# Hashed attention with a mixture of adapters: q and k turned by VectorE and by DMAs that move partitions, in place of TensorE transposes

## The chip, the cores and the metric

The kernel runs on one core of a Trainium2 chip. A core has five engines with queues of their own: TensorE (PE; its weight loads are listed as PEld), VectorE (DVE), ScalarE (ACT), GpSimd (POOL), and SyncE (SP), which here only issues transfers. PE writes its products to PSUM, a small memory of eight banks; everything else lies in SBUF, 128 partitions wide. Each engine executes its instructions in the order of its queue, and waits at an instruction until what that needs is there.

The metric is the time on the device in microseconds (us). All times below are of one core.

## The reference

There are two stages. The first is attention in which a query sees only the keys with the same hash. For 4 batches and 8 heads, 768 positions and 64 features:

```
bit    = (q . proj > 0)            6 bits each for q and for k; the 6 bits are the bucket
scores = q . k^T / 8               where the buckets are equal, else -1e9
attn   = softmax(scores)
out    = attn . v
```

The outputs of the 8 heads are put side by side: 3,072 rows of 512. The second stage routes each row to two of eight small adapters of rank 16:

```
logits = x @ w_gate ;  top 2 of 8 ;  w = exp(logit - max) / (sum + 1e-9)
out    = x + sum over the two of  w * ((x @ A[e]) @ B[e])
```

## The kernel before

The work is cut into 16 **head pairs** (two heads of one batch, numbered p), four to a batch. A pair's scores are a matrix of 768 keys by 768 queries for each of two heads, computed as nine **tiles** of 1,024 columns (`score`, s = 0 to 8). The equality of buckets is folded into the same product: `aug` holds, for q and for k, 64 rows of features and below them six rows of bits as plus or minus one half, and a constant row, so that one product with 71 rows gives the score less a large number where bits differ. ACT turns each tile from PSUM (two buffers, `ps_s`) into exponentials, `P`, in bf16 (line 193). `pvmm` then multiplies `P` with v (and a column of ones for the sum), and `norm` divides (lines 223 and 225) into `x`.

`aug` must have features on partitions, while q and k come from memory with positions on partitions. So each pair needs these steps, done one pair ahead:

- `load` (SP): q, k and v of a pair, 384 KB each. Partition number is position divided by six.
- `trans`, three times: four TensorE transposes of 128 by 128 in fp32 into one PSUM buffer (`ps_t`, two of them; line 144), and a DVE copy into `qkT` (line 147).
- `hash`: four products of `qkT` with the projection into one PSUM buffer (line 155), a DVE step that makes signs of them (`sgn`, line 158), and eight DMAs on SP that put the six bit rows of each of four parts into `aug` (line 164).
- `cast`, twice: DVE scales half of `qkT` and writes it to `aug` as bf16 (line 172).

There are two `aug` buffers, so the one for pair p+1 is filled while the scores of pair p are computed. GpSimd casts v to bf16 (`vcast`) and `x` to `xb` (line 229).

When a batch is done, the adapters follow: `xtrans` (TensorE transposes of `xb`, and a copy), `lgz` (logits and `x @ A` in one product), `route` (a chain of some ten short DVE steps and one exponential), `zmtrans`, and six times `delta` (a product with B, line 301, a DVE step that scales and adds, line 303, and every second time a store to memory). All of these share one PSUM buffer, `ps_m`.

The order is written out by hand in `run`: for each pair the nine score tiles, and after each tile some of the other work, for the pair before (values, normalisation), for the pair after (turning, hashing) and, through `moe_slot`, for the last batch. Each engine's queue has the instructions in that order. DVE's first work in a pair is the first normalisation of the pair before, `norm(p - 1, 0)`, and then the copies for pair p+1. SP has, for each pair, the three loads of pair p+2, then the eight bit DMAs of pair p+1, and in some pairs stores.

Of the kernel before, what the change touches and what calls it, by code (L numbers as in the profile page):

```python
# [19 lines left out]
class Emitter:  # L20


    def __init__(self, ctx, tc, q, k, v, proj, w_gate, A, Bm, out):
# [21 lines left out]
        self.qktp = ctx.enter_context(tc.tile_pool(name="qktp", bufs=2))  # L45
# [6 lines left out]
        self.ps_s = ps("ps_s", 2)  # L52
        self.ps_t = ps("ps_t", 2)
# [10 lines left out]
        self.proj2 = sg.tile([P, 32], F32, name="proj2")  # L64
        nc.vector.memset(self.proj2, 0.0)
        nc.sync.dma_start(out=self.proj2[0:64, 0:6], in_=proj)
        nc.sync.dma_start(out=self.proj2[64:128, 6:12], in_=proj)
# [5 lines left out]
        for i in range(2):  # L73
            a = sg.tile([P, 4, S], BF16, name=f"aug{i}")
            for h in range(2):
                nc.vector.memset(a[64:96, 2 * h, :], 1.0)
                nc.vector.memset(a[64:96, 2 * h + 1, :], -1.5)
            self.aug.append(a)
# [13 lines left out]
        self.nat, self.vn, self.qkT, self.sgn, self.P_, self.pv = {}, {}, {}, {}, {}, {}  # L92
# [13 lines left out]

    def load(self, p):
# [4 lines left out]
        n = self.natp.tile([self.P, 2, 2, self.T * self.D], F32, tag="nat", name=f"nat{p}")  # L112
        for i, src in enumerate((self.q, self.k)):
            nc.sync.dma_start(out=n[:, i], in_=src[b, h:h + 2].rearrange(
                "h (p t) d -> p h (t d)", t=self.T))
# [18 lines left out]

    def trans(self, p, g):
        if p >= self.n_pairs:
            return
        nc, P, D = self.nc, self.P, self.D
        if g == 0:
            self.qkT[p] = self.qktp.tile([P, 2 * self.S], F32, tag="qkT", name=f"qkT{p}")  # L140
        ps = self.ps_t.tile([P, 512], F32, tag="t", name=f"tr{p}_{g}")
        for j in range(4):
            idx, u = divmod(4 * g + j, 3)
            nc.tensor.transpose(out=ps[:, j * P:(j + 1) * P],  # L144
                                in_=self.nat[p][:, idx % 2, idx // 2, u * P:(u + 1) * P],
                                identity=self.ident)
        nc.vector.tensor_copy(out=self.qkT[p][:, g * 512:(g + 1) * 512], in_=ps)  # L147

    def hash(self, p):
        if p >= self.n_pairs:  # L150
            return
        nc = self.nc
        ps = self.ps_t.tile([self.P, 384], F32, tag="t", name=f"hs{p}")
        for j in range(4):
            nc.tensor.matmul(out=ps[32 * j:32 * j + 32, :], lhsT=self.proj2,  # L155
                             rhs=self.qkT[p][:, j * 384:(j + 1) * 384], start=True, stop=True)
        sgn = self.sgp.tile([self.P, 384], BF16, tag="sgn", name=f"sgn{p}")
# [3 lines left out]
        for j in range(4):  # L161
            av = aug[64:70, j, :].rearrange("p (u e c) -> p u e c", e=2, c=self.P)
            for e in range(2):
                nc.sync.dma_start(out=av[:, :, e, :],  # L164
                                  in_=sgn[32 * j + 6 * e:32 * j + 6 * e + 6, :].rearrange(
                                      "p (u c) -> p u c", c=self.P))

    def cast(self, p, e):
        if p >= self.n_pairs:
            return  # L170
        av = self.aug[p % 2][0:64].rearrange("p j (u e c) -> p (j u) e c", e=2, c=self.P)
        self.nc.vector.tensor_scalar(  # L172
            out=av[:, :, e, :],
            in0=self.qkT[p][64 * e:64 * e + 64, :].rearrange("p (j c) -> p j c", c=self.P),
            scalar1=2.0 ** -5, scalar2=None, op0=ALU.mult)


    def score(self, p, s):
# [6 lines left out]
        while at < end:  # L185
# [4 lines left out]
            nc.tensor.matmul(out=ps[:, o:o + n], lhsT=aug[0:71, 2 * h + 1, kt * P:(kt + 1) * P],  # L190
                             rhs=aug[0:71, 2 * h, q0:q0 + n], start=True, stop=True)
# [104 lines left out]
    def delta(self, b, i):  # L296
# [8 lines left out]
        if i % 2 == 1:  # L305
            S = self.S
            nc.sync.dma_start(
                out=self.out[b * S:(b + 1) * S, :].rearrange("(p t) f -> p t f", t=self.T)[:, i - 1:i + 1, :],
                in_=self.acc[b][:, i - 1:i + 1, :])


    def moe_slot(self, p, s):
        o = p - 2
        if o >= 0 and o % self.PPB == 0 and o // self.PPB >= 1:
            b = o // self.PPB - 1
            if s in (1, 3):
                self.lgz(b, s // 2)
            if s in (2, 4):
                self.route(b, s // 2 - 1)
            if s == 5:  # L320
                self.zmtrans(b)
        o = p - 3
        if o >= 0 and o % self.PPB == 0 and o // self.PPB >= 1:
            b = o // self.PPB - 1
            if s < 6:
                self.delta(b, s)

    def run(self):
# [3 lines left out]
        for g in range(3):  # L332
            self.trans(0, g)
        self.hash(0)
        self.cast(0, 0)
        self.cast(0, 1)
        self.vcast(0)
        self.load_moe()
        self.trans(1, 0)
        for p in range(N):  # L340
            for s in range(9):
                self.score(p, s)
                if s == 0:
                    self.load(p + 2)
                    self.norm(p - 1, 0)
                    self.trans(p + 1, 1)
                if s == 1:
                    self.trans(p + 1, 2)
                    self.vcast(p + 1)
                if s == 2:  # L350
# [79 lines left out]
```

The softmax here doesn't subtract the row's maximum and nothing guards it: scores larger than these inputs give would overflow.

## Time and profile before

| | |
|---|---|
| three runs, median | 218.93 us (218.74 to 220.49) |
| the profiled execution | 218.24 us, of which its span is 216.4 |
| PE clock granted, mean | 0.925 |
| ACT starts its first score tile | 18.83 |
| ACT ends its last score tile | 191.76 |
| PE / DVE / ACT / POOL busy | 178.0 / 142.9 / 144.1 / 63.4 us |
| ACT's wait for score tiles | 43.6 us |

The span is the time from the first to the last instruction in the trace; the rest of the device's time lies around it. Lines of the profile name an engine, a line of the code (L193 is line 193), an operation, what it writes and reads (`P<-s`), the shapes, how often it ran, its busy time and the mean duration of one in ns. Behind that stands the time for which the engine had been idle just before, with the instruction that released it. `SPq` is SP issuing a DMA; a line `DMA` in the chain of waits is the time until the data landed. Busy times overlap between engines, so a share says little by itself: what bounds a stretch is the engine for which the others wait there.

### The profile page before, as it was taken

Reading aid. Unit: us, or ns where it says so; the run is one execution under the profiler, and the core shown is the slowest. Engines: PE = TensorE matmul, PEld = TensorE weight load, DVE = VectorE, ACT = ScalarE, POOL = GpSimd, SP = SyncE. Lnnn points to the kernel's source line nnn. Section 1 sums busy time; section 2 is a strip of 40 time slices with the busy share of each in tenths; the row PEclk is TensorE's granted clock in tenths of the full one; section 3 lists DMA queues with packets and bytes.
Section 4 is the critical chain, followed back from the end, with each engine's and each line's share of the span. In section 5 each row is a group of like instructions: output and inputs, shape, how many; then the busy total and the mean of one; then the engine's idle time right before and its main releaser. Section 6 shows DMA issues by size and latency. Waiting matters only on the chain.

```text
span 216.4 us, 5569 instructions
## 1 busy us (share of the span) xinstructions
PE 178.0 (82%) x2288; PEld 123.5 (57%) x2288; DVE 142.9 (66%) x303; ACT 144.1 (67%) x153; POOL 63.4 (29%) x98
## 2 busy tenths in 40 slices
PE   1647999999999997998979987989999879774341
PEld 0314286865868674756656866657678656463200
DVE  7771528675686768698756689796766875634541
ACT  2003679998999987677969976868999858730000
POOL 1694420623416050604133503305144110101000
PEclk9995569999999999999999999999999999997555
DMA  5895406062442616180746042533815000420024
GB/s 144 293 25 82 169 11 217 9 224 71 160 156 76 224 22 209 9 309 11 253 168 215 15 152 76 191 132 141 283 46 186 3 9 3 197 100 0 0 118 173
DMA packets 22874, 26.39 MB, mean 122 GB/s; under 512 B 8897, under 2 KB 21313, under 8 KB 22849
## 3 DMA queue, kind: packets, MB, share of 16 engines
q1 hardware_dynamic: 18016, 25.77, 35.2%
q0 software_dynamic: 4832, 0.27, 3.9%
q8 instruction: 18, 0.29, 0.6%
q14 instruction: 8, 0.06, 0.1%
HBM read 19.42 MB, written 6.29 MB: 119 GB/s over the span
## 4 chain that ended last, share of the span: by engine, by line
PE 52%; DVE 22%; DMA 9%; SPq 8%; issue 5%; ACT 2%; POOLq 0%; POOL 0%; DVEq 0%
PE s L190 20%; PE pv L209 12%; SPq L164 7%; PE tr L144 7%; PE hs L155 5%; DVE acc L303 5%; DMA nat<-in_k_dram 5%; PE dl L301 3%; DMA aug<-sgn 3%; DVE aug L172 3%; DVE sgn L158 2%; PE xtp L238 2%; DVE zm L276 2%; DMA nat<-in_q_dram 2%; DVE x L225 2%
## 5 line engine op out<-in xcount | busy, mean ns | idle before, releaser
L193 ACT ACTIVATE P<-s 128x1024 bf16<-128x1024 f32 x144 | 141.6, 1024 | 47.1 <-PE s L190 43.6
L190 PE MATMUL s<-aug 71*128 71x512 bf16 (+1 forms) x384 | 89.9, 336 | 5.0 <-DMA aug<-sgn 4.8
L209 PEld LDWEIGHTS <-P 128*128 128x128 bf16 x1152 | 51.3, 98 | 14.8 <-DVE x L225 1.0
L209 PE MATMUL pv<-vb,P 128*128 128x65 bf16 x1152 | 53.8, 194 | 0.9 <-DVE x L225 0.9
L190 PEld LDWEIGHTS <-aug 71*128 71x128 bf16 x384 | 32.5, 100 | 28.8 <-issue 13.0
L229 POOL CAST xb<-x 128x768 bf16<-128x768 f32 x16 | 13.2, 825 | 115.3 <-DVE x L225 115.3
L147 DVE COPY qkT<-tr 128x512 f32<-128x512 f32 x48 | 33.0, 690 | 14.1 <-PE tr L144 12.5
L144 PE MATMUL tr<-ident,nat 128*128 128x128 f32 x192 | 32.9, 296 | 8.1 <-DMA nat<-in_q_dram 3.9
L209 PE MATMUL pv<-vb,eps 128*128 128x65 bf16 x192 | 37.4, 195 | 0.0
L144 PEld LDWEIGHTS tr<-ident,nat 128*128 128x128 f32 x192 | 25.2, 152 | 14.4 <-issue 5.6
L172 DVE TENSOR_SCALAR aug<-qkT 64x1536 bf16<-64x1536 f32 x32 | 31.9, 998 | 0.9
L223 DVE RECIPROCAL ri<-pv 128x6 f32<-128x6 f32 x32 | 6.2, 193 | 29.5 <-PE pv L209 29.4
L303 DVE SCALAR_TENSOR_TENSOR acc<-dl,rt,x 128x512 f32<-128x512 f32 x24 | 17.9, 745 | 6.0 <-PE dl L301 6.0
L209 PEld LDWEIGHTS <-eps 128*128 128x128 bf16 x192 | 18.9, 98 | 0.0
L225 DVE TENSOR_TENSOR x<-pv,ri 128x384 f32<-128x384 f32 x32 | 17.8, 557 | 1.2
L126 POOL CAST vb<-vn 128x768 bf16<-128x768 f32 x16 | 13.3, 833 | 13.7 <-DMA vn<-in_v_dram 13.7
L128 POOL TENSOR_TENSOR vs<-vn 128x384 f32<-128x384 f32 x16 | 16.7, 1044 | 0.0
L301 PE MATMUL dl<-Bcat,zmT 128*128 128x512 bf16 x24 | 10.3, 431 | 7.7 <-DVE acc L303 6.8
L155 PE MATMUL hs<-qkT,proj 128*32 128x384 f32 x128 | 15.8, 542 | 0.0
L158 DVE TENSOR_SCALAR sgn<-hs 128x384 bf16<-128x384 f32 x16 | 8.9, 558 | 8.6 <-PE hs L155 7.0
L250 PE MATMUL lz<-wa,xT 128*128 128x136 bf16 x96 | 7.7, 235 | 4.3 <-DVE zm L276 3.6
L238 PE MATMUL xtp<-ident_bf,xb 128*128 128x128 bf16 x96 | 8.0, 219 | 3.0 <-POOL xb L229 1.4
(35 smaller groups left out, 79.6 us busy)
## 6 DMA issues: line engine op xcount, KB each, us to landing
nat<-in_q_dram SPq DMA_DIRECT2D x16, 384.0 KB
nat<-in_k_dram SPq DMA_DIRECT2D x16, 384.0 KB
vn<-in_v_dram SPq DMA_DIRECT2D x16, 384.0 KB
out_dram<-acc SPq DMA_DIRECT2D x12, 512.0 KB
aug<-sgn SPq DMA_DIRECT2D x128, 4.5 KB
wa<-in_moe_A_dram POOLq DMA_DIRECT2D x4, 32.0 KB, 3.1
Bcat<-in_moe_B_dram POOLq DMA_DIRECT2D x1, 128.0 KB, 3.5
proj<-in_proj_dram SPq DMA_DIRECT2D x2, 1.5 KB
```

What stands on the lines that cost most here:

```text
L128: nc.gpsimd.tensor_add(out=s3, in0=vn[:, :, 0:3, :], in1=vn[:, :, 3:6, :])
L144: nc.tensor.transpose(out=ps[:, j * P:(j + 1) * P], in_=self.nat[p][:, idx % 2, idx // 2, u * P:(u + 1) * P], identity=self.ident)
L147: nc.vector.tensor_copy(out=self.qkT[p][:, g * 512:(g + 1) * 512], in_=ps)
L155: nc.tensor.matmul(out=ps[32 * j:32 * j + 32, :], lhsT=self.proj2, rhs=self.qkT[p][:, j * 384:(j + 1) * 384], start=True, stop=True)
L164: nc.sync.dma_start(out=av[:, :, e, :], in_=sgn[32 * j + 6 * e:32 * j + 6 * e + 6, :].rearrange("p (u c) -> p u c", c=self.P))
L172: self.nc.vector.tensor_scalar(out=av[:, :, e, :], in0=self.qkT[p][64 * e:64 * e + 64, :].rearrange("p (j c) -> p j c", c=self.P), scalar1 ...
L190: nc.tensor.matmul(out=ps[:, o:o + n], lhsT=aug[0:71, 2 * h + 1, kt * P:(kt + 1) * P], rhs=aug[0:71, 2 * h, q0:q0 + n], start=True, stop=True)
L193: nc.scalar.activation(out=self.P_[p][:, s * 1024:end], in_=ps, func=ACT.Exp, scale=128.0)
L209: nc.tensor.matmul(out=pv[:, i, :], lhsT=lhsT, rhs=vb[:, h, kt, :], start=(kt == 0), stop=(kt == T))
L225: nc.vector.tensor_tensor(out=self.x[b][:, :, c:c + D], in0=pv[:, :, 0:D], in1=ri.unsqueeze(2).to_broadcast([P, T, D]), op=ALU.mult)
L301: nc.tensor.matmul(out=ps, lhsT=self.zmT[b][:, i * P:(i + 1) * P], rhs=self.Bcat, start=True, stop=True)
L303: nc.vector.scalar_tensor_tensor(out=self.acc[b][:, i, :], in0=ps, scalar=self.rt[b][:, i:i + 1], in1=self.x[b][:, i, :], op0=ALU.mult, op ...
```

## The change

q and k are loaded with 12 neighbouring positions on a partition, the first head on partitions 0 to 63, the second on 64 to 127. `trans` is one DVE transpose for q and one for k, which turns each 32 by 32 block in its place and writes position order with a step of 12. `hash` multiplies the result with a projection laid out four times over (`proj4`), summing two products of 32 features. `cast` moves to GpSimd, which writes bf16 to a new tile `cb`; after the second cast of a pair, eight DMAs on SP bring blocks of 32 partitions to their place in `aug`. The bits go by four DMAs instead of eight. Positions in `aug` are now in natural order, so the score product reads its weights, the keys, with a step of six, and the output is stored with 128 rows to a block.

The PSUM buffers of `trans` go, and there are three score buffers; `hash` uses `ps_m`. In `run`, `trans` and `cast` stand behind tiles 0 and 1, the values of the second head behind tiles 1 to 3, `hash` behind tile 4, `xtrans` comes a pair earlier, and the adapters of a batch are spread over three pairs instead of two.

```diff
-        self.qktp = ctx.enter_context(tc.tile_pool(name="qktp", bufs=2))
+        self.tbp = ctx.enter_context(tc.tile_pool(name="tbp", bufs=2))
...
-        self.ps_s = ps("ps_s", 2)
-        self.ps_t = ps("ps_t", 2)
+        self.ps_s = ps("ps_s", 3)
...
+        for b in range(4):
+            nc.scalar.dma_start(out=pst[32 * b:32 * b + 32], in_=proj.rearrange("(d r) n -> r d n", d=2))
+        for b in range(4):
+            nc.vector.tensor_copy(out=self.proj4[32 * b:32 * b + 32, :, b:24:4], in_=pst[32 * b:32 * b + 32])
...
             nc.sync.dma_start(out=n[:, i], in_=src[b, h:h + 2].rearrange(
-                "h (p t) d -> p h (t d)", t=self.T))
+                "h (p t) d -> (h p) (t d)", t=2 * self.T))
...
+    def trans(self, p, i):
+        nc, P, T2 = self.nc, self.P, 2 * self.T
+        if i == 0:
+            self.tb[p] = self.tbp.tile([P, 2, 2, 32 * T2], F32, tag="tb", name=f"tb{p}")
+        nc.vector.transpose(
+            out=self.tb[p][:, :, i, :].rearrange("p d (c t) -> p t d c", t=T2),
+            in_=self.nat[p][:, i, :].rearrange("p (t d r) -> p t d r", t=T2, d=2))
+
+    def cast(self, p, i):
+        nc, P, T2 = self.nc, self.P, 2 * self.T
+        if i == 0:
+            self.cb[p] = self.tbp.tile([P, 2, 2, 32 * T2], BF16, tag="cb", name=f"cb{p}")
+        nc.gpsimd.tensor_scalar(out=self.cb[p][:, :, i, :], in0=self.tb[p][:, :, i, :],
+                                scalar1=2.0 ** -5, scalar2=None, op0=ALU.mult)
+        n = 32 * T2
+        if i == 1:
+            for d in range(2):
+                for b in range(4):
+                    h, b2 = divmod(b, 2)
+                    nc.sync.dma_start(
+                        out=self.aug[p % 2][32 * d:32 * d + 32, :, h, b2 * n:b2 * n + n],
+                        in_=self.cb[p][32 * b:32 * b + 32, d])
+
     def hash(self, p):
+        n = 16 * 2 * self.T
+        ps = self.ps_m.tile([P, n], F32, tag="m", name=f"hs{p}")
+        for d in range(2):
+            for g in range(4):
+                i, half = divmod(g, 2)
+                nc.tensor.matmul(out=ps[32 * g:32 * g + 32, :], lhsT=self.proj4[:, d, :],
+                                 rhs=self.tb[p][:, d, i, half * n:half * n + n],
+                                 start=(d == 0), stop=(d == 1))
...
+        for g in range(4):
+            i, half = divmod(g, 2)
+            nc.sync.dma_start(
+                out=aug[64:70, i].rearrange("r h (b x) -> r (h b) x", b=2)[:, :, half * n:half * n + n],
+                in_=sgn[32 * g:32 * g + 24, :])
...
-            nc.tensor.matmul(out=ps[:, o:o + n], lhsT=aug[0:71, 2 * h + 1, kt * P:(kt + 1) * P],
-                             rhs=aug[0:71, 2 * h, q0:q0 + n], start=True, stop=True)
+            nc.tensor.matmul(out=ps[:, o:o + n], lhsT=aug[0:71, 1, h, bass.ds(kt, P, step=self.T)],
+                             rhs=aug[0:71, 0, h, q0:q0 + n], start=True, stop=True)
...
     def moe_slot(self, p, s):
+        for k in (1, 2, 3):
+            o = p - k
+            if o < 0 or o % self.PPB != self.PPB - 1:
+                continue
+            b = o // self.PPB
+            if k == 1 and s == 5:
+                self.lgz(b, 0)
+                self.route(b, 0)
+            if k == 2 and s == 0:
+                self.lgz(b, 1)
+                self.route(b, 1)
+            if k == 2 and s == 5:
                 self.zmtrans(b)
+            if k == 3 and s in (0, 1, 2, 3, 5, 6):
+                self.delta(b, (0, 1, 2, 3, 5, 6).index(s))
...
                 if s == 0:
                     self.load(p + 2)
                     self.norm(p - 1, 0)
+                    self.trans(p + 1, 0)
+                    self.cast(p + 1, 0)
+                if s in (1, 2, 3):
+                    self.pvmm(p - 1, 1, 2 * s - 2, 2 * s)
+                if s == 1:
                     self.trans(p + 1, 1)
+                    self.cast(p + 1, 1)
+                if s == 3:
+                    self.norm(p - 1, 1)
+                if s == 4:
+                    self.hash(p + 1)
+                    self.vcast(p + 1)
+                if s == 5:
+                    self.xtrans(p - 1)
+                if s in (6, 7, 8):
+                    self.pvmm(p, 0, 2 * s - 12, 2 * s - 10)
                 self.moe_slot(p, s)
```

## The prediction

> **What bounds the kernel now.** I read the busy times first, then the costliest groups, then stretches of the loop by engine, then the chain of waits. Busy times and groups:
>
> ```profile
> PE 178.0 (82%) x2288; PEld 123.5 (57%) x2288; DVE 142.9 (66%) x303; ACT 144.1 (67%) x153; POOL 63.4 (29%) x98
> ...
> L193 ACT ACTIVATE P<-s 128x1024 bf16<-128x1024 f32 x144 | 141.6, 1024 | 47.1 <-PE s L190 43.6
> ...
> L126 POOL CAST vb<-vn 128x768 bf16<-128x768 f32 x16 | 13.3, 833 | 13.7 <-DMA vn<-in_v_dram 13.7
> L128 POOL TENSOR_TENSOR vs<-vn 128x384 f32<-128x384 f32 x16 | 16.7, 1044 | 0.0
> ```
>
> ACT waits 43.6 us for score tiles, so PE sets the pace. The stretches (busy by engine, then PE clock, DMA share, GB/s) are two plain head pairs of the loop, and the start:
>
> ```profile
> 13.20:17.20 4.00, 0.00 (x0) 0.03 (x1) 3.10 (x3) 0.00 (x0) 4.00 (x5) 0.94 1.42 36
> 17.20:22.00 4.80, 4.39 (x16) 2.71 (x17) 1.30 (x2) 2.05 (x2) 1.35 (x3) 0.50 0.47 113
> 22.00:26.00 4.00, 4.00 (x17) 1.24 (x16) 2.44 (x4) 2.43 (x3) 1.24 (x2) 0.50 0.51 191
> ...
> 50.80:59.80 9.00, 9.00 (x135) 6.62 (x134) 5.98 (x11) 8.59 (x9) 2.76 (x4) 1.00 0.43 137
> 59.80:69.00 9.20, 9.20 (x136) 6.74 (x135) 6.48 (x11) 8.61 (x10) 3.46 (x6) 1.00 0.40 135
> ```
>
> In a plain pair PE has no gap (9.00 of 9.00), but ACT is nearly full too: nine tiles back to back take 9.04 us (54.77 to 63.81 in the timeline). So taking work from PE can win a plain pair almost nothing. What lies above 9.04 is elsewhere: counted by ACT's tiles, the loop runs from 18.83 to 191.76, 172.9 us; pair 0 takes 13.1 and the pairs that carry adapter work 11 to 13. The third thing is how close pair 3 came to being late, in the chain of waits:
>
> ```profile
> 44.38 0.57 DVE sgn L158
> 44.95 0.02 issue
> 44.97 0.76 SPq L164
> 45.73 0.05 issue
> 45.78 0.73 SPq L164
> 46.51 0.05 issue
> 46.56 0.72 SPq L164
> 47.29 0.04 issue
> 47.33 3.07 DMA aug<-sgn
> 50.40 0.05 issue
> 50.45 0.28 PE s L190
> ```
>
> SP issues one sign DMA each 0.775 us, and the fourth lands 3.07 us after its issue began: the next pair's scores already wait for it. Loads are cheaper on the same queue (start to start 0.49 to 0.56):
>
> ```profile
> 51.22 0.44 SPq L114 DMA_DIRECT2D nat<-in_q_dram  x1
> 51.71 0.46 SPq L114 DMA_DIRECT2D nat<-in_k_dram  x1
> ```
>
> **The change by parts.** *PE.* Twelve transposes per head pair go, four of them 0.44 us in the chain, so 1.32 us: PE's work in a plain pair, W, falls from 9.0 to 7.7. Hashing streams as many columns as before. The score weights are now read with a step of six elements; no row has that. Bounds: nothing, or, by the fp32 weight load (140 ns against 98), 24 x 0.05 = 1.2 us per pair. I take nothing, since weight loads run beside matmuls.
>
> *DVE.* Per pair three copies (0.69) and two casts (0.95) go, 4.0 us, and two transposes of 128x768 fp32 come. Bounds for one: 0.55 (the cast's 954 ns for 1536 elements, halved, and a start) and 1.75 (a 512-element copy out of PSUM takes 0.69, so 768 take 0.95; that with the scattered write costing as much again). I take 0.95. DVE is free for a third of a plain pair, so its total is worth nothing; its place in order is what counts.
>
> *POOL.* Two casts of 768 elements per pair: 0.83 by its own cast, 2.1 by its two-input row (1.044 for 384). I take 0.83; they fit (POOL is busy 3 to 4 of 9 us).
>
> *SP.* Eight sign DMAs become four, still onto six rows (0.775 each), and eight partition-moving DMAs come, of 32 rows. Bounds 0.43 (the v load, 0.41, plus the gap) and 0.775; I take the loads' 0.49, since their shape is nearest. Per pair 8 x 0.49 + 4 x 0.775 + 1.5 for loads = 8.5 us: below the period, but serial. Data: 393 KB more per pair beside 1,180 KB that keep the DMA engines 40% busy; hidden. Loads in runs of 3,072 bytes and stores in runs of 2,048 I count at nothing, beside the same 40%.
>
> *Moves.* Hashing now takes the one small PSUM buffer, which the x transposition also uses one slot later: the sign step (about 0.4) releases it during a score tile of 0.44, so 0 to 0.4, and I take 0. The x transposition comes a pair earlier, two slots after the value products end: normalisation 0.78 and POOL's cast 0.83 need 1.6 us, and PE has 2.2 us of work between. Nothing, as long as POOL is not behind.
>
> **The new path.** All twelve DMAs must land before the pair's first score. They begin with DVE's transposes, which stand in DVE's order behind the first normalisation of the pair before, and that waits for PE's last matmuls of that pair. From there, L:
> - normalisation 0.20 + 0.56 and gaps: 0.83
> - two transposes: 1.98 with gaps
> - second POOL cast: 0.93
> - eight issues on SP: 3.92
> - three sign issues 2.33, the fourth's issue and landing 3.07, and the semaphore 0.05
> - sum **L = 13.1 us**; low ends together 11.5, high ends 18.5.
>
> The old path had only three issues before its last one. Call S(p) the start of pair p's scores on PE. S(p) + W is where PE ends pair p; there the normalisation begins, and L with it, for pair p+2. So S(p+2) is the later of S(p+1) + W and S(p) + W + L: two pairs cost 7.7 + 13.1 = 20.8, or 10.4 each, with PE idle 5.4 us in every second pair. The three score buffers don't help, since what they would hold is not computed yet. Behind SP's wait for POOL's cast stand the sign DMAs and the next loads (loads are a pair ahead, so nobody misses them); behind PE's wait at the first score stand the value products and the next hashing.
>
> *Adapter pairs*, three batches. In the first of the three pairs PE has 1.4 us more (a routing product 0.71, and a wait for the copy before it 0.65). In the second, routing stands on DVE between the two transposes and waits for a product behind the first score: S + 0.45 + 0.71 + 2.06 (routing, as in the tail, 197.6 to 199.6) + 0.95 + 0.93 + 3.92 + 2.33 + 3.12 = 14.5 from one start to the next, with no second pair to share it. In the third, the first accumulation (0.38 + 0.75) stands there instead and two output issues (0.45 each) come before the signs: 13.8.
>
> Intervals: pair 0 13.1 as before; 13.1, 7.7, 13.1; then 9.1, 14.5, 13.8, 8.3; then 12.5, 14.5, 13.8, 8.3; then 12.5, 14.5, 13.8, and 9.0 for the last, which ACT bounds. (8.3 and 12.5 follow from the rule: the third adapter pair's W is 9.0, so 9.0 + 13.1 - 13.8 = 8.3 and 20.8 - 8.3 = 12.5.) Sum 191.6, against 172.9: **+18.7**.
>
> *Start.* DVE is free at 8.0; small copies for the projection 0.4 (estimate from the 0.09 us memset), transposes to 10.3, cast to 11.2, SP to 15.1, landing at 20.6, first tile at half clock 1.06: ACT starts at 21.7 instead of 18.83, **+2.8**. *Tail*: one transposition of x leaves it, but it ran while PE waited for the last normalisation; 0.
>
> *Clock.* After PE idled 4.0 us (13.2 to 17.2) its clock was 0.50 until about 30, and pair 0 took 4 us more than others; a 1.6 us idle at 110 left the clock at 1.00. The new stalls are 5 us. If each costs the next pair 4 us, the same intervals give +17 instead of +0 (adapter pairs absorb most). I take a quarter, **+4**: behind the stalls work is dense, at the start it was not. The Trainium skill (TensorE: Matmul & The Clock Gate, Part 1) says idle of about 3.4 us halves the clock and as long a busy stretch restores it; the row's low clock lasted longer. By that rule a stalled pair loses about 1.7 us, +7 in all, an estimate from the page.
>
> Sum: the profiled execution took 218.24 (span 216.4), 0.3% under the median 218.93. 218.24 + 18.7 + 2.8 + 4 = **244**.
>
> A rule of the skill speaks against the change: the SBUF Cachelines section of Advanced Engine Details and Errata wants two accesses in each 16-byte line. The transposes write at a step of 48 bytes and the score weights are read at 12. No row here shows either; by the rule both lean to their upper ends.
>
> **Rivals.**
> - *Dear steps* (chance 0.20): SP's new issues cost the signs' 0.775. L becomes 15.3, and some ten intervals lengthen by about 2: 264. With slow transposes, casts or weight loads more, to 283. For it: both sides of these DMAs are in SBUF, as with the signs. Against: 32 rows, not six.
> - *Cheap steps* (0.14): every low end, no clock loss. L = 11.5; by the same rule 220 to 228, the start still later.
> - *ACT becomes the bound: faster* (0.14). If the path hides, PE's 1.32 us and the third buffer let ACT run at 9.04 in every pair: 13.1 + 15 x 9.04 = 149 and some 4 for adapter pairs, 20 less than 172.9, with the start +2.8: about 201. It decides where W + L falls under two ACT periods, L < 10.4; that needs 2.7 us out of 13.1, for example a transposition that doesn't wait behind the normalisation. For it: ACT waits 43.6 us in all now. Against: even the low ends give 11.5.
> - *PE isn't relieved* (inside the first): strided weights add 1.2 to W, 0.6 per pair: 251.
> - The forecast, 230 to 256: 0.52.
>
> The range 217 to 268 leaves out most of the fast case and the dearest ends. Faster by over 1%: 0.13; within 1%, which is about what a measurement of this kernel can't tell from no change, 0.05; slower 0.82.
>
> **What would show it.** ACT's wait for scores should grow from 43.6 to some 70 us, released through the sign DMA; PE should show idle stretches near 5 us at the first score of pairs 2, 4 and 6, with SP busy in the three to seven us before. DVE's transposes should stand directly behind the normalisation, at 0.95; SP's new issues at 0.49. If PE instead runs through and ACT's tiles follow each other at 1.0, the path was shorter than I summed, and the prediction is wrong on the other side.

## The result, and the profile after

The changed kernel takes 301.91 us (median of four runs, 300.15 to 305.6) against 219.06 for the kernel before: a ratio of 1.374, with a 95% interval of 1.364 to 1.384. The forecast was 244 with a range up to 268, so the direction was right and the size far off. The profiled execution took 305.6 us with a span of 303.5: it is the slowest of the four (the others took 300.15 to 302.54, at a slightly higher clock), so the times inside it, used below as they stand, come to some 4 us too much.

First the page of the changed kernel: busy times, the clock that PE was granted in 40 slices, and the groups that answer to those shown of before.

```profile
PE 200.0 (66%) x2224; PEld 134.2 (44%) x2224; DVE 122.7 (40%) x255; ACT 144.0 (47%) x153; POOL 129.6 (43%) x130
...
PEclk9999995558955886795695965978995976959655
...
L203 ACT ACTIVATE P<-s 128x1024 bf16<-128x1024 f32 x144 | 141.2, 1026 | 121.4 <-PE s L200 121.0
L200 PE MATMUL s<-aug 71*128 71x512 bf16 (+1 forms) x384 | 113.1, 416 | 52.0 <-DMA aug<-sgn 52.0
L153 POOL TENSOR_SCALAR cb<-tb 128x768 bf16<-128x768 f32 x32 | 68.1, 2129 | 106.2 <-DVE tb L142 76.4
```

ACT still works 141 us on its tiles, but waits 121.0 us for scores instead of 43.6. PE waits 52.0 us in front of its scores for the bits that the sign DMA brings, 12.4 of them before its first score. It has fewer instructions than before and yet is busy 22 us longer, because the clock stands at 0.5 to 0.8 in many slices. At the start the line of the clock misleads: it shows 9, but in pair 0 six products with v took 0.54 us, as in the later stretches at 0.50, where the same six take 0.35 at full clock. A GpSimd cast takes 2.13 us where 0.83 was taken.

The stretches of the loop (length, then busy time by engine with counts, PE clock, DMA share, GB/s), from one pair's first score to the next:

```profile
39.20:56.60 17.40, 11.20 (x134) 7.73 (x132) 8.67 (x12) 9.16 (x10) 9.27 (x8) 0.72 0.29 85
56.60:71.00 14.40, 14.39 (x131) 9.25 (x132) 1.67 (x4) 8.52 (x9) 6.18 (x7) 0.51 0.43 134
71.00:88.00 17.00, 8.50 (x136) 6.14 (x133) 8.60 (x12) 9.11 (x10) 11.33 (x9) 0.90 0.28 76
```

Two pairs alternate, as forecast, but not as cheaply. In the first and the third, PE stands still for 6.2 and 8.5 us: 2.3 and 2.5 in the middle of the pair, waiting for `xb`, and 3.9 and 6.0 before the next pair's scores. In the one between, PE is busy for 14.39 of 14.40 us, at a clock of 0.51: it runs through the pair at half speed. 14.39 times 0.51 is 7.3 us of full-speed work. The clock had fallen before the stall at the score: in pair 1 it is 1.00 up to 46.9, where the wait of 2.3 us ends, and 0.50 from there on.

The chain of waits shows the stalled pair 3, from its normalisation to the scores of pair 4 (start, length, what):

```profile
71.18 0.21 DVE ri L233
...
71.89 1.56 DVE tb L142
73.45 0.08 issue
73.53 1.98 POOL cb L153
75.50 0.23 issue
75.73 2.13 POOL cb L153
77.86 0.06 issue
77.92 0.83 POOL xb L239
78.76 0.05 issue
78.80 0.51 PE xtp L248 x6
...
85.23 0.71 SPq L183
85.95 0.04 issue
85.99 1.90 DMA aug<-sgn
87.89 0.09 issue
87.98 1.03 PE s L200 x3
```

Two casts stand in series on GpSimd, and behind them the cast `xb`, for which PE waits in the middle of the pair (the transposition of x). SP's line in the timeline shows the rest:

```profile
77.89 5.61 SPq L160 DMA_DIRECT2D aug<-cb  x8
83.60 3.11 SPq L183 DMA_DIRECT2D aug<-sgn  x4
```

The eight moves start 0.03 us behind the second cast, the four sign DMAs directly behind the moves.

Measured against the forecast, from score to score (the last to the end of ACT's tiles), in us:

| intervals | forecast | measured | difference |
|---|---|---|---|
| pair 0 | 13.1 | 11.6 | -1.5 |
| stalled plain pairs 1, 3 | 26.2 | 34.4 | +8.2 |
| plain pair behind a stall, 2 | 7.7 | 14.4 | +6.7 |
| first of the adapter's three, 4, 8, 12 | 34.1 | 47.0 | +12.9 |
| second, 5, 9, 13 | 43.5 | 53.4 | +9.9 |
| third, 6, 10, 14 | 41.4 | 53.1 | +11.7 |
| the pairs behind them, 7, 11, 15 | 25.6 | 36.7 | +11.1 |
| sum | 191.6 | 250.6 | +59.0 |

Besides, ACT starts its first tile at 28.7 instead of the forecast 21.7.

### The profile page after: what moved, and what is told of

Same layout as the page of the kernel before. It is cut to its first block, busy times and chain, and to the rows that moved or that the text cites. A ratio compares the mean times of both kernels' runs of the same rounds, so it can differ in the third digit from the quotient of the medians.

```text
span 303.5 us, 5560 instructions
## 1 busy us (share of the span) xinstructions
PE 200.0 (66%) x2224; PEld 134.2 (44%) x2224; DVE 122.7 (40%) x255; ACT 144.0 (47%) x153; POOL 129.6 (43%) x130
## 4 chain that ended last, share of the span: by engine, by line
PE 37%; SPq 15%; DVE 14%; POOL 14%; DMA 9%; issue 8%; ACT 0%; ACTq 0%; POOLq 0%; DVEq 0%
PE s L200 16%; PE pv L219 9%; POOL cb L153 9%; SPq L183 8%; SPq L160 6%; DMA aug<-sgn 6%; DVE tb L142 4%; PE lz L260 3%; PE dl L311 3%; PE xtp L248 3%; DVE acc L313 3%; PE hs L174 3%; POOL xb L239 2%; DMA pst<-in_proj_dram 2%; DVE zm L286 1%
## 5 line engine op out<-in xcount | busy, mean ns | idle before, releaser
L203 ACT ACTIVATE P<-s 128x1024 bf16<-128x1024 f32 x144 | 141.2, 1026 | 121.4 <-PE s L200 121.0
L200 PE MATMUL s<-aug 71*128 71x512 bf16 (+1 forms) x384 | 113.1, 416 | 52.0 <-DMA aug<-sgn 52.0
L153 POOL TENSOR_SCALAR cb<-tb 128x768 bf16<-128x768 f32 x32 | 68.1, 2129 | 106.2 <-DVE tb L142 76.4
L200 PEld LDWEIGHTS <-aug 71*128 71x128 bf16 x384 | 42.2, 136 | 77.8 <-issue 56.3
L219 PEld LDWEIGHTS <-P 128*128 128x128 bf16 x1152 | 66.5, 114 | 21.7 <-issue 12.4
L219 PE MATMUL pv<-vb,P 128*128 128x65 bf16 x1152 | 68.8, 215 | 0.9 <-DVE x L235 0.9
L142 DVE STREAM_TRANSPOSE tb<-nat 128x768 f32<-128x768 f32 x32 | 47.0, 1511 | 0.0
L174 PE MATMUL hs<-tb,proj 128*32 128x192 f32 x256 | 18.8, 394 | 16.1 <-DVE ident_bf L61 12.3
L313 DVE SCALAR_TENSOR_TENSOR acc<-dl,rt,x 128x512 f32<-128x512 f32 x24 | 17.9, 746 | 15.3 <-PE dl L311 15.3
L174 PEld LDWEIGHTS hs<-tb,proj 128*32 128x32 f32 x256 | 8.1, 124 | 27.3 <-DVE ident_bf L61 12.3
L250 DVE COPY xT<-xtp 128x768 bf16<-128x768 bf16 x16 | 8.9, 558 | 27.2 <-PE xtp L248 27.2
L235 DVE TENSOR_TENSOR x<-pv,ri 128x384 f32<-128x384 f32 x32 | 17.8, 557 | 1.1
L248 PEld LDWEIGHTS <-xb 128*128 128x128 bf16 x96 | 7.4, 114 | 19.8 <-POOL xb L239 18.2
```

Source lines behind the costliest of these rows:

```text
L142: nc.vector.transpose(out=self.tb[p][:, :, i, :].rearrange("p d (c t) -> p t d c", t=T2), in_=self.nat[p][:, i, :].rearrange("p (t d r) -> ...
L153: nc.gpsimd.tensor_scalar(out=self.cb[p][:, :, i, :], in0=self.tb[p][:, :, i, :], scalar1=2.0 ** -5, scalar2=None, op0=ALU.mult)
L174: nc.tensor.matmul(out=ps[32 * g:32 * g + 32, :], lhsT=self.proj4[:, d, :], rhs=self.tb[p][:, d, i, half * n:half * n + n], start=(d == 0) ...
L200: nc.tensor.matmul(out=ps[:, o:o + n], lhsT=aug[0:71, 1, h, bass.ds(kt, P, step=self.T)], rhs=aug[0:71, 0, h, q0:q0 + n], start=True, stop ...
L203: nc.scalar.activation(out=self.P_[p][:, s * 1024:end], in_=ps, func=ACT.Exp, scale=128.0)
L219: nc.tensor.matmul(out=pv[:, i, :], lhsT=lhsT, rhs=vb[:, h, kt, :], start=(kt == 0), stop=(kt == T))
```

## The experiments

The kernels fall in three groups: terms of the operand path (the way from `nat` to `aug`), that path taken out of the way, and what was then left over. Times are medians, with the lowest and highest of the runs where they are far apart.

### Terms of the path

**Casts on VectorE** (e1_cast_dve).

```diff
-        nc.gpsimd.tensor_scalar(out=self.cb[p][:, :, i, :], in0=self.tb[p][:, :, i, :],
+        nc.vector.tensor_scalar(out=self.cb[p][:, :, i, :], in0=self.tb[p][:, :, i, :],
```

> The two casts of a pair run on VectorE instead of GpSimd; nothing else changes. In the changed kernel the path from the normalisation to the next-but-one pair's first score took 17.2 us (39.4 to 56.6 for pair 2), of which GpSimd's two casts in series hold 4.3. Theory 1 (the serial path behind the normalisation sets the time): a VectorE cast should take about 0.5, the path falls to 14.5, two pairs fall by 2.7, and the time goes from 301 to about 280. Theory 2 (PE's low clock sets the time, the path is secondary): under 8 us gained. Theory 3 (GpSimd is the culprit as an engine, its 2.13 us casts also hold up the x cast): more than 35 us gained.

Measured: 282.24, 20 less, as theory 1 has it. The group of this kernel:

```profile
L153 DVE TENSOR_SCALAR cb<-tb 128x768 bf16<-128x768 f32 x32 | 18.2, 568 | 1.1
```

The same operation takes 0.57 us on VectorE and 2.13 on GpSimd. Pair 1 takes 16.3 instead of 17.4. Having the casts on GpSimd makes some 20 of the 83 us.

**Dense transposes** (e5_dense_write): the transposes write block behind block, not with a step of 12 elements. That puts the positions in another order, so the kernel attends to permuted positions; every instruction is still there.

```diff
-            out=self.tb[p][:, :, i, :].rearrange("p d (c t) -> p t d c", t=T2),
+            out=self.tb[p][:, :, i, :].rearrange("p d (t c) -> p t d c", t=T2),
```

> VectorE's transposes write their blocks densely (a step of 4 bytes) instead of with a step of 48 bytes. Positions are then in another order, so keys no longer stand with their values: that part of the computation is changed, the work is the same in kind and amount. If the scattered write is what makes a transpose 1.51 us instead of the 0.95 that I took, the row falls to about 0.95, the path by 0.5 to 1.1 and the time by 4 to 9 us. If the transpose itself costs it, the row stays at 1.5 and the time at 301.

Measured: 290.29 (one run, beside 300.15 to 305.6), some 11 less, where 4 to 9 were expected.

```profile
L142 DVE STREAM_TRANSPOSE tb<-nat 128x768 f32<-128x768 f32 x32 | 29.9, 957 | 0.0
```

A transpose takes 0.96 us where it writes densely and 1.51 with the step of 48 bytes. The forecast's 0.95 was right for the work of a transpose, and the scattered write costs 0.55 on top. The Trainium skill (Advanced Engine Details and Errata, SBUF Cachelines) speaks against such a step; the runs agree, on the writing side. On the reading side, a load of the score weights, with its step of 12 bytes, took 0.126 us against 0.098 before, both at full clock (e11 and before, medians of a plain pair); it runs beside the products, and the shortest of these stayed at 0.27 us.

**Two score buffers** (e4_two_buffers).

```diff
-        self.ps_s = ps("ps_s", 3)
+        self.ps_s = ps("ps_s", 2)
```

> The changed kernel with two score buffers instead of three. By the theory that PE waits for operands that don't exist yet, the third buffer is worth nothing here: 301, within 3. If it lets ACT run on through PE's stalls, two buffers cost up to 1 us a stall, some 8 to 10 us in all.

Measured: 300.97, the same. In this kernel the third buffer is worth nothing. What its two banks were worth elsewhere is another question, which came up last.

**PE kept warm** (e3_warm): two score buffers, and 20 products of 512 columns between pairs that nobody reads.

```diff
+            if p < N - 1:
+                ps = self.ps_j.tile([self.P, 512], F32, tag="j", name=f"j{p}")
+                for _ in range(20):
+                    self.nc.tensor.matmul(out=ps, lhsT=self.eps, rhs=self.fill, start=True, stop=True)
```

> Two score buffers, and in the PSUM bank that this frees 20 products of 512 columns without use, 4.3 us at full clock, between the last product of a pair and the first score of the next. The path for the operands is untouched. If the low clock is what the stalls cost beyond their length, the clock should rise from 0.79 to above 0.95, W fall from some 14 to 9, and two pairs take 17.2 + 9 = 26 instead of 31.6: about 262 us. If the clock plays no part, the products only add to PE's work: 300 or more.

Measured: 296.58, 5 less, where about 262 was expected if the clock carries the loss. The mean clock went from 0.77 in the profiled execution to 0.93, and plain pairs 1 to 3 took 13.4, 12.9 and 12.8, 39.1 together instead of 48.8. But the first three pairs with adapter work took 14.5, 18.0 and 17.0 (15.3, 17.8 and 17.9 in the changed kernel), and pair 0, where the products only get in the way, 16.2 instead of 11.6. Against e4, which also has two score buffers and whose pairs 1 to 3 took 45.4 together, the gain there is 6.3. So the low clock costs 2 to 3 us in each of these pairs; pairs 2 and 3 took 25.7 where 26 were expected for two. In the adapter pairs little came of it: the longest two of each batch are set by a chain from start to start, and where PE has no gap, the 20 products themselves take some 4.3 us (11 in a row took 2.54). So the run gives a lower bound of what the clock costs, and shows that the clock alone doesn't carry the loss.

### The path out of the way

**Turned and cast earlier** (e2_early): transposes and casts of pair p+2 behind tiles 5 and 6 of pair p, the moves in a step of their own.

```diff
                 if s == 0:
-                    self.trans(p + 1, 0)
-                    self.cast(p + 1, 0)
+                    self.move(p + 1)
...
+                if s in (5, 6):
+                    self.trans(p + 2, s - 5)
+                    self.cast(p + 2, s - 5)
```

> The transposes and casts of pair p+2 stand behind tiles 5 and 6 of pair p, ahead of the normalisation, and the eight partition-moving DMAs of pair p+1 behind tile 0 of pair p; all work is the same. Theory 1 (the path begins at the normalisation because of the order): transposes and casts leave the path; what is left is SP's queue, 1.4 for loads, 5.3 for moves, 3.2 for signs, so some 9.8 us a pair, and about 220 us in all. Theory 2 (low PE clock by itself): PE has no long waits left, so the clock returns to 1.0 and this too gives about 220; the run doesn't separate them, the granted clock with e3_warm does. Theory 3 (total GpSimd or VectorE work too large): stays above 270.

Measured: 257.28, 45 less, but far from the 220 expected. PE still waited for the sign DMA:

```profile
PE s L203 <- DMA aug<-sgn: 35.3, 10, 11.8
```

(The columns of this list are us in total, times, the longest.) Two GpSimd casts of 2.13 end only just before SP needs them, and eight moves and four sign issues still stand between there and the score.

**A whole pair ahead** (e6_ahead): three `aug` buffers, all the preparation of pair p+2 done in pair p, behind tiles 1 to 4, casts on VectorE, and loads three pairs ahead into a fourth buffer.

```diff
-        for i in range(2):
+        for i in range(3):
             a = sg.tile([P, 2, 2, S], BF16, name=f"aug{i}")
...
                 if s == 4:
-                    self.hash(p + 1)
+                    self.hash(p + 2)
...
+                if s in (1, 2):
+                    self.trans(p + 2, s - 1)
+                    self.cast(p + 2, s - 1)
+                if s == 3:
+                    self.move(p + 2)
```

> Everything that readies a pair's operands comes a whole pair earlier: transposes and casts of pair p+2 behind tiles 1 and 2 of pair p, casts on VectorE, three operand buffers so that the moves don't wait for the scores, moves behind tile 3, hashing of p+2 behind tile 4. SP keeps all transfers: 1.4 + 5.3 + 3.2 and some 0.3 for stores, 10.2 us a pair. Theory 1 (a serial path that is too long to hide; total work fits): the waits of PE go, the clock stays near 1.0, and SP's queue becomes the bound, some 10.2 a pair: 215 to 228. Rival (GpSimd, VectorE or DMA work too large in total, whatever the order): above 245.

Measured: 257.1, another miss of mine, and the one that turned the study. PE's waits at the scores fell to

```profile
L203 PE MATMUL s<-aug 71*128 71x512 bf16 (+1 forms) x384 | 97.4, 368 | 3.5 <-DMA aug<-sgn 3.5
```

3.5 us in all, at the start of the kernel. The operand path was gone, and 38 us over the kernel before were left: adapter pairs of 15.5 and 17.3 us with a clock of 0.78 and 0.70, plain pairs of 9.8. The time lies where the rival had it (above 245, too much work in total), but the rival isn't the cause: e12 below has the same work in another order and with other buffers, and takes 207.51.

**Loads on another queue** (e7_loads_pool): e6 with the loads issued by GpSimd from pair 3 on.

```diff
+        q = nc.sync if p < 3 else nc.gpsimd
```

> As e6_ahead, with the loads of q, k and v from pair 3 on issued by GpSimd, so SP has 8.7 us a pair. If SP's queue bounds e6_ahead, ACT is the next bound at 9.05 a pair, and the time falls by some 12 to 17 us against e6_ahead, to 200 to 212, faster than before the change. If not, the two are within 4 us.

Measured: 254.77 (254.33 to 255.49). SP's queue was not the rest.

**The start** (e8_start): e7 with the constants of `aug` and the copies of the projection on GpSimd, so that VectorE can turn at once.

```diff
-            nc.vector.tensor_copy(out=self.proj4[32 * b:32 * b + 32, :, b:24:4], in_=pst[32 * b:32 * b + 32])
+            nc.gpsimd.tensor_copy(out=self.proj4[32 * b:32 * b + 32, :, b:24:4], in_=pst[32 * b:32 * b + 32])
...
-            nc.vector.memset(a[64:96, 0], 1.0)
-            nc.vector.memset(a[64:96, 1], -1.5)
+            nc.gpsimd.memset(a[64:96, 0], 1.0)
+            nc.gpsimd.memset(a[64:96, 1], -1.5)
```

> As e7_loads_pool, with the constants of the operand buffers and the four copies of the projection written by GpSimd, so that VectorE's first transpose doesn't stand behind them. The first transpose began at 10.7 us; it should begin near 5, when q has landed, and the whole should gain 4 to 6 us against e7_loads_pool. If the start is bound by SP's twelve issues rather than by VectorE, the gain is the same, as they follow; if by the constants themselves on GpSimd, there is none.

Measured: 244.11 (242.58 to 245.93), a gain of 10.7 where 4 to 6 were expected. The first transpose begins at 4.3, ACT's first tile at 20.5. In the changed kernel VectorE turned the first tile only at 10.71, behind the constants and the copies of the projection, and these wait for four small DMAs.

### What was left: 25 us in the adapter pairs

The list of waits of e8_start, below its largest lines:

```profile
PE xtp L252 <- POOL xb L243: 11.7, 14, 1.8
PE hs L178 <- DVE tb L143: 11.0, 16, 2.1
PE dl L315 <- DVE acc L317: 10.0, 9, 1.4
```

and one adapter pair in PE's timeline (start, length, instruction, in brackets the idle time before it and its releaser):

```profile
77.76 0.52 PE L178 MATMUL hs<-tb,proj 128*32 128x192 f32 x4 [0.41 <-DVE tb L143]
...
79.78 0.84 PE L178 MATMUL hs<-tb,proj 128*32 128x192 f32 x12 [1.50 <-DVE tb L143]
...
81.95 0.82 PE L252 MATMUL xtp<-ident_bf,xb 128*128 128x128 bf16 x6 [0.77 <-POOL xb L243]
...
83.42 0.80 PE L304 MATMUL ztp<-ident_bf,zm 128*128 128x128 bf16 x6 [0.65 <-DVE xT L254]
```

None is long. They add up to 3.3 us within 6, and from 82 on the clock is 0.50 (stretches of 2 us):

```profile
80.00:82.00 2.00, 1.24 (x16) 0.53 (x9) 1.24 (x4) 0.77 (x1) 0.93 (x2) 0.92 0.10 24
82.00:84.00 2.00, 1.35 (x12) 1.19 (x13) 0.56 (x1) 0.25 (x1) 1.92 (x3) 0.50 0.31 73
84.00:86.00 2.00, 2.00 (x21) 1.40 (x19) 0.56 (x1) 0.89 (x1) 1.92 (x5) 0.50 0.41 100
```

Two parts of the change could make them: where it puts the adapter's work and the x transposition, and that `hash`, the x transposition, routing and accumulations now share one PSUM buffer.

**Placement, first try** (e9_place): e8 with `moe_slot` and the x transposition as before; I also moved the preparation to tiles 5 to 8, and `hash` back to one pair ahead.

```diff
-                if s == 3:
+                if s == 8:
                     self.move(p + 2)
...
-                if s == 5:
-                    self.xtrans(p - 1)
+                if s == 6:
+                    self.xtrans(p - 2)
```

> Keeps the kernel's preparation ahead of time (casts on VectorE, three aug buffers, loads on GpSimd's queue, constants on GpSimd), and puts back where the kernel before had it: the adapter's spread over two pairs, and the x transposition two pairs behind. Theory (the rest of the loss is the adapter's new placement: TensorE waits for hash on a turned tile, for the x cast, for the accumulation, each followed by a lower clock): plain pairs fall from 9.8 to 9.1 to 9.4, adapter pairs from 11.3, 15.9 and 17.5 to about 13 and 12, and the total from 244.1 to 216 to 225, beside the 219 of before. Rival (VectorE's extra work or a lower clock whatever the placement): 238 or more. Third possibility, the placement is half of it: 226 to 237.

Measured: 261.33 (259.27 to 270.51), slower by 17. It doesn't tell what it was made for, since the later preparation brought stalls back (the longest of this kernel, from PE's timeline):

```profile
55.93 1.03 PE L204 MATMUL s<-aug 71*128 71x512 bf16 x3 [8.35 <-DMA aug<-cb]
```

SP's last sign DMA for these scores was issued by 49.98. Why the wait lasted until 55.9 stays open; three loads of 384 KB were issued at 48.6 to 50.4.

**The adapter's place alone, in the changed kernel** (e10_adapter_back).

```diff
-            if k == 1 and s == 5:
-                self.lgz(b, 0)
-                self.route(b, 0)
...
+            if s in (1, 3):
+                self.lgz(b, s // 2)
+            if s in (2, 4):
+                self.route(b, s // 2 - 1)
...
-                if s == 4:
+                if s == 3:
                     self.hash(p + 1)
```

> The changed kernel with the adapter's place put back alone (logits, routing and the zm transposition in pairs 6, 10 and 14, delta and its accumulation in 7, 11 and 15, and the next pair's hash a step earlier), the path of the operands left. Theory (the adapter's pairs are slow because routing and accumulation stand between the transpositions and the casts of the next pair): the starts of those pairs go from 17.8 apart to the plain mean of about 15.8, which is 10 to 16 less: 285 to 292. Rival (the operand path alone sets the pair, whatever stands beside it): 298 to 303.

Measured: 296.24, 5.7 less: between the two cases, so a part, and a small one while the operand path stands.

**Placement, cleanly** (e11_ahead_place): e8 with only the adapter and the x transposition moved back, `hash` behind tile 5.

> The kernel with everything prepared a whole pair ahead (244.1), its order of preparation left as it is (transpositions and casts behind the second and third tile, moves behind the fourth), and only the adapter's work put back where the kernel before had it, with the x transposition two pairs behind (and hash a tile later, to keep the small PSUM buffer free for routing). The run e9 had also moved the preparation later, and stalls at the first scores came back there, so it couldn't tell. Theory (placement): no wait at the first scores, plain pairs 9.2 to 9.5 instead of 9.8, three adapter pairs 35 to 38 together instead of 44.7: 214 to 226. Rival (placement worth nothing once the operands are early): 238 to 250.

Measured: 236.0 (231.4 to 237.77), 6 to 13 less than e8, between the two cases. Plain pairs fell to 8.7 us, less than the 9.04 I had held for ACT's least. But the first adapter pairs still took 18.7 and 17.2:

```profile
82.81 0.88 PE L264 MATMUL lz<-wa,xT 128*128 128x136 bf16 x12 [2.63 <-DVE zm L290]
...
87.25 1.51 PE L178 MATMUL hs<-tb,proj 128*32 128x192 f32 x16 [1.98 <-DVE ss L295]
89.23 0.80 PE L304 MATMUL ztp<-ident_bf,zm 128*128 128x128 bf16 x6 [0.47 <-DVE sgn L182]
```

Here each wait is for the small buffer: the second logits wait until routing has read the first ones, `hash` until routing is through, the next transposition until the signs are made.

**The banks given back** (e12_own_banks): e11 with two score buffers, and the two banks used for a hash buffer and a second small one.

```diff
-        self.ps_s = ps("ps_s", 3)
+        self.ps_s = ps("ps_s", 2)
...
-        self.ps_m = ps("ps_m", 1)
+        self.ps_m = ps("ps_m", 2)
+        self.ps_h = ps("ps_h", 1)
...
-        ps = self.ps_m.tile([P, n], F32, tag="m", name=f"hs{p}")
+        ps = self.ps_h.tile([P, n], F32, tag="h", name=f"hs{p}")
```

> The same kernel with two score buffers instead of three, and the two PSUM banks set free given to a hash buffer of its own and a second small buffer. Theory (sharing one small buffer among hash, x transposition, routing and accumulation is part of the adapter pairs' length, TensorE waited 10.0 us for accumulations): 3 to 9 less than e11_ahead_place, all of it in adapter pairs, and 208 to 220 in all. Rival (third score buffer needed now, or sharing harmless): the same within 2, or more.

Measured: 207.51 (207.27 to 214.38), 28 less than e11 (24 between the lowest runs of the two) where 3 to 9 were expected, and faster than the kernel before: ratio 0.953, interval 0.944 to 0.962; every run lies below the lowest run of before beside it, 215.89. A plain pair and the first two adapter pairs of e12:

```profile
57.40:66.40 9.00, 8.36 (x131) 6.41 (x132) 6.19 (x10) 8.24 (x10) 5.31 (x9) 1.00 0.57 176
75.30:87.70 12.40, 10.36 (x163) 7.88 (x160) 10.01 (x33) 8.96 (x12) 6.73 (x12) 1.00 0.54 151
87.70:101.20 13.50, 11.23 (x143) 7.50 (x141) 10.39 (x16) 8.90 (x10) 5.88 (x9) 0.87 0.61 178
```

and the same two adapter pairs of e11:

```profile
76.00:94.70 18.70, 13.63 (x166) 9.71 (x163) 10.82 (x33) 9.17 (x12) 7.69 (x13) 0.73 0.54 168
94.70:112.00 17.30, 13.94 (x143) 8.48 (x140) 10.56 (x16) 9.01 (x10) 5.21 (x8) 0.70 0.44 145
```

The adapter pairs fall from 18.7 and 17.3 to 12.4 and 13.5 at an almost full clock: where the waits for the buffer go, the low clock goes too. The 10.9 us between the spans of e12 (205.5) and before (216.4) are 5.7 in the loop (167.2 against 172.9), 5.8 in the tail (18.9 against 24.7, where the small buffer is needed most), less 0.6 of a later start. The tail is the last batch's adapter work, which uses the small buffer throughout; so about half of the gain seems to be not the turning of q and k but the second small buffer that it leaves room for. No run parts the two.

**The banks alone, in the changed kernel** (e13_banks_alone): the edit of e12 on the changed kernel.

> The changed kernel with the PSUM banks given back alone: two score buffers, a buffer of its own for hash, two small buffers; the operand path as the change has it. Theory A (the operand path sets the pairs first, and sharing the small buffer costs only where that path is out of the way): 285 to 302. Theory B (sharing the small buffer is itself most of the loss, and the path lies beside it): 245 to 275.

Measured: 293.71 (290.97 to 298.41), 4 to 11 less. Its PE still waits for the bits:

```profile
PE s L201 <- DMA aug<-sgn: 64.1, 13, 12.1
```

That is theory A: while the operand path sets the pairs, the shared buffer costs little.

**The banks without the placement** (e15_ahead_banks): the edit of e12 on e8.

> The kernel prepared a whole pair ahead with the adapter and the x transposition where the change put them (244.1), and the banks given back. Together with e11_ahead_place (236.0) and e12_own_banks (207.5) it parts placement from sharing: if the shared buffer is the cause, whatever the placement: 210 to 222, plain pairs still 9.5 to 9.8 for the x transposition's wait; if placement and sharing only count together: 232 to 242.

Measured: 227.27 (220.7 to 229.83), 14 to 23 less than e8; the median lies between the cases, the lowest run (the profiled one) in the first, the shared buffer as the cause whatever the placement. Plain pairs stay at 9.8, for the x transposition's wait. Its batches differ from each other: 11.3, 13.1 and 12.1 us in the first, 11.3, 15.2 and 12.2 in the second, and in the pairs that took 13.1 and 15.2 the mean clock was 0.87 and 0.78. The same work loses more or less by the clock from batch to batch.

From e8 on, then: placement alone 6 to 13, banks alone 14 to 23, both 36.6. By the lowest runs of e11 and e15 (12.7 and 23.4 less) they add up; by the medians they help each other, and the spread leaves that open.

## Why the prediction was wrong

The mechanism was seen rightly: the twelve DMAs on the path before a pair's first score, stalls in every second plain pair, released through the sign DMA. The step that failed first is the size of that path, L: 13.1 was taken and 16.8 measured, mostly because GpSimd's casts, priced at 0.83, took 2.13 and both stood on it, and because the eight moves took 5.74 instead of 3.92. Put into the forecast's own rule, the measured lengths (16.8 for L, 17.8 and 17.7 for the second and third adapter pair, 11.6 for pair 0) give 226.5 us of intervals instead of 191.6. That is an estimate; it leaves 24 of the measured 250.6 for the clock and whatever else, where 4 were allowed. Step by step:

- **PE's work, W = 7.7: right.** 7.3 by the stretch at half clock. Loading weights with a step of six elements takes longer (0.126 us against 0.098), but beside the products, as forecast.
- **The path, L = 13.1: too short; measured 16.8** from the normalisation in pair 3 to the first score of pair 4. The normalisation and gaps took 0.71 (0.83 taken). Transposes and casts took 5.97 (2.91): the transposes 1.51 instead of 0.95, and casts 2.13 instead of 0.83, so that both casts, 4.3 us, stand on the path and not the second alone. The moves took 5.74 (3.92): 0.65 to 0.70 each instead of 0.49. Three sign issues 2.39 (2.33). The last one's issue and landing 1.90 (3.07). With the semaphore 0.09 that is 16.8. The bounds were also added up a little wrongly: by the forecast's own terms the low ends give some 11.8 and the high ends some 18.3, not 11.5 and 18.5. For the cast I took GpSimd's plain cast, which has one input like the new step; but the new step multiplies, and it took what the two-input row gave as the upper bound (2.1). For the moves I took the loads' 0.49 rather than a value between the bounds, and for the landing the one row that before had.
- **Adapter pairs, 14.5 and 13.8: too short by 3.3 and 3.9**, by the same terms.
- **Clock, +4 of a possible +17: too low.** The row of the kernel's start (half speed for 13 us behind 4 us of idling) was nearer the truth, and my reason to discount it, that the work behind a stall is dense, is refuted: pair 2 was dense, busy 14.39 of 14.40 us, and stayed at 0.51. It took 14.4 instead of 7.7, 6.7 lost, where I had allowed 4 at most for a stall. In this execution the clock had fallen in pair 1 already, behind the wait for `xb`; in e1 that wait was 0.8 us, and behind a stall of 6.3 pair 2 was again busy 14.27 of 14.30 us at 0.51. The Trainium skill (TensorE: Matmul & The Clock Gate, Part 1) would have the clock back after about 3.4 busy us; these runs contradict that, and the measurement decides. How long the low clock lasts varies: in e4 pair 2 was at 0.50 for its first 6.4 us and took 13.0. In the changed kernel pair 7, behind the adapter's three, was dense as well (12.81 of 13.0 us busy) and took 13.0 at 0.60 where 8.3 was forecast.
- **x transposition a pair earlier, "nothing, as long as POOL is not behind": the condition failed.** The chain shows POOL's casts of `tb` in front of `xb` and PE behind it. In e8, with the casts gone from GpSimd, PE still waited 11.7 us in 14 pairs.
- **Hash on the small PSUM buffer, 0 to 0.4 per pair, 0 taken: wrong.** I priced it against the x transposition in a plain pair and never against routing and accumulation, which hold the same buffer too: in e11 one `hash` waited 1.98 us for routing. A buffer of its own for `hash`, together with a second small one, was worth 4 to 11 us in the changed kernel and 14 to 28 once the path is out of the way; what the sharing with `hash` costs by itself no run parts.
- **Third score buffer nothing: right** (e4), but in the account as a free addition. It was paid with two banks.
- **ACT's least, 9.04 per plain pair: misread.** The nine tiles from 54.77 to 63.81 weren't back to back: where one follows another at once, their starts lie 0.90 to 0.92 apart, but three of these steps were 1.12 to 1.17. e11's plain pairs took 8.7. So relieving PE could win a plain pair more than I allowed.
- **Start, +2.8: measured +9.9.** I had VectorE free at 8.0; it began at 10.71. Slower transposes, two slow casts and dearer moves make the rest.
- **Tail 0: right** (25.2 against 24.7).

The sum of the profiled executions: 218.24 to 305.6 is +87.4, of it +9.9 start, +76.7 loop, +0.5 tail and 0.3 around the span. The forecast had +2.8, +22.7 (with the clock) and 0. Of the rivals, *dear steps* was nearest (264 to 283), yet the L of its upper end, 18.5, was above the measured one: even that end lacked most of the clock, the start and the buffer. *ACT becomes the bound* named its condition rightly, L hidden, "for example a transposition that doesn't wait behind the normalisation": e6 met it, and it didn't suffice. With the start, the adapter's place and the banks changed too, e12 came to 207.5, near that rival's 201.

## What to carry to other kernels

Price an operation by what it does to each element on that engine, not by the engine's cheapest row of the same shape, and sum a serial path of small transfers with every issue. When a change frees or takes a shared buffer, list everybody who uses that buffer and how long each holds it: waits of one or two us in a row can cost more by the lowered clock than by themselves (in the two adapter pairs of e11 against e12, 4.1 us of idle time and 6.0 of longer work). A cause that lies beside a longer one shows little when it alone is undone (e10, e13: 4 to 11 us; with the path gone, 6 to 28), so take the longest away first.

## What the runs showed of the hardware

- GpSimd scaled 128x768 fp32 to bf16 in 2.13 us, while its plain cast of the same size took 0.83; VectorE did the former in 0.57.
- A 32x32 transpose of 128x768 fp32 took 0.96 us with dense writes and 1.51 with writes 48 bytes apart.
- A load of weights of 71 rows by 128 in bf16 took 0.126 us with a step of 12 bytes and 0.098 dense; beside the products it showed no cost.
- SP's issue took 0.59 to 0.70 us for 32 rows from SBUF to SBUF, 0.71 to 0.79 for the bits onto six rows, and mostly 0.42 to 0.44 for loads of 128 rows.
- PE ran whole pairs without a gap at half clock behind a stall (14.39 of 14.40 us busy at 0.51 in the changed kernel, 14.27 of 14.30 at 0.51 in e1); in other places the clock was back within 7 us (e4's pair 2; half from 82 to 88 in e8, then 0.88). No run here shows what decides between them.
